# Three plain attention batches ahead of the feed-forward, the third one's x parked in DRAM, and w_out decoded straight to DRAM

## The chip, the cores and the metric

The kernel runs on one core of a Trainium2 chip. The metric is the device time of one execution in microseconds (us); the kernel before has a median of 1222.8 us over three runs. The engines are TensorE (PE in the profile; its weight loads are PEld), VectorE (DVE), ScalarE (ACT), GpSimd (POOL) and SyncE (SP), which starts most DMAs. Each engine works through its own queue in order. SP is such a queue too: a DMA that waits for something holds back every DMA written behind it.

## The reference

Sigmoid attention over 8 batches of 12 heads, 448 positions of 64 numbers, and a feed-forward on the joined result:

```python
scores = scale * np.matmul(q, k.transpose(0, 1, 3, 2)) - np.log(S)
attn_out = np.matmul(1.0 / (1.0 + np.exp(-scores)), v)           # 8 x 12 x 448 x 64
x = attn_out.transpose(0, 2, 1, 3).reshape(B * S, H * D)          # 3584 x 768
h = x @ w_in                                                      # w_in: 768 x 2048
g = 0.5 * h * (1.0 + erf(h * inv_sqrt2))
out = g @ w_out                                                   # w_out: 2048 x 768
```

q, k and v are float32. The weights arrive as float64 bit patterns and have to be turned into float32 on the chip; the text calls this decoding.

## The kernel before

**Blocks.** The 3584 tokens are done as seven blocks of T = 512: the 448 tokens of one batch and 64 of the eighth, whose x is made first and kept in DRAM (`scr_x`). A block is `ffn1` (L433), the first products h with Gelu: 16 slices `fc` of 18 matmuls each, and `ffn2` (L460), the second products: 6 output slices of 16 steps, each step 3 matmuls, 288 in all. Every product is made of three fp32r matmuls, of high and low parts (`wl xh`, `wh xl`, `wh xh`). So each weight unit is split into high and low by one ACT cast (L226) and one DVE subtraction (L227), into the tile `whl`. There are 16 units of `w_in` (768 columns) and 12 of `w_out` (1024 columns, called out 0 to out 11 here, two to each output slice).

**Attention.** Batches 0 to 2 (`PLAIN = 3`; batch 0 is the eighth batch of the input) are done with plain float32 matmuls (`scores_plain` L333, `values_plain` L349), pair of heads by pair of heads; the later ones with split operands (`scores` L281, `values` L376). Before the first block `attention_first` (L398) does batches 0 and 1, so 12 pairs. The attention of batch t + 2 is mixed into `ffn2` of block t by `window` (L490): it makes some score or value matmuls and then lets so many steps of `ffn2` run (`until`), and so on. The text calls such an excursion of TensorE into attention and back a visit. Batch 2, the last plain one, is done in this way in block 0, in 12 halves of a pair. x of the next block goes to `xh` and `xl`, which `ffn1` has finished reading by then. The tokens of the eighth batch are read back from `scr_x` by `load_tokens` (L371).

**Decoding.** The generator `decoder` (L87) cuts the weights into 40 chunks: 16 of w_in, one to a unit (768 KB of float64 each), then 24 of w_out, two to a unit (512 KB). For a chunk i it does `start(i)` (three DVE instructions, L117 to L122), `scale(i)` (two on ACT, L130 and L133) and, one chunk later, `end(i)` (two on DVE, L138 and L147, the last of which writes the float32 weights). Straight after `end(i - 1)` it asks for the raw data of chunk i + 2 (L110, on SP); there are three raw buffers. `W.decode(n)` moves the generator on to two half steps for each chunk of n. After `decode(n)` chunk n - 1 is started and chunk n - 2 ended. Three numbers set the pace, `PACE_A, PACE_F, PACE_W = 14, 8, 24`: 14 during `attention_first`, 8 during the first `ffn1`, the rest during block 0's window. The float32 units of w_in stand in the buffers that g takes later (`first_w`), those of w_out in the three buffers of the tag `wst`. In block 0 both are split from there. They are also stored to DRAM (`scr_in` by SP, `scr_out` by POOL, L190, a whole unit at a time), from where the later blocks read them back into `wst` (`load_to`, L197 to L212).

**Order of preparing.** `prepare_to` (L214) splits the next unit; with the beginning of unit u, unit u + 1 is split, into the buffer that unit u - 1 has just left (`whl` has two in block 0). So the ACT cast of unit u + 1 waits until TensorE has finished unit u - 1, and TensorE waits at the beginning of unit u + 1 for the DVE subtraction. In DVE's queue this subtraction stands between the decoding steps written before and behind it.

Of the kernel before, what the change touches and what calls it, by code (L numbers as in the profile page):

```python
# [17 lines left out]
P = 128  # L18
# [4 lines left out]
def tile_sigmoid_attention_gelu_ffn(  # L23
# [45 lines left out]
    scr_out = tc.dram_tile([NO, P, NFH * P], F32, name="scr_out")  # L69
    scr_x = tc.dram_tile([2, P, NPAIR, S], F32, name="scr_x")  # L70
    WU = max(NC, NFH) * P


    PLAIN = 3
    PACE_A, PACE_F, PACE_W = 14, 8, 24
    SUB_IN, SUB_OUT = NC * P, NFH * P // 2
    SUB = max(SUB_IN, SUB_OUT)
    KEPT = 4
# [8 lines left out]
    def decoder():  # L87
# [47 lines left out]
        def end(i):  # L135
            high = raws.pop(i)[:, :, 1]
            m, e = parts.pop(i)
            nc.vector.scalar_tensor_tensor(  # L138
                e, high, 0x80000000, e, op0=ALU.bitwise_and, op1=ALU.bitwise_or
            )  # L140
            kind, u, c0, w = chunks[i]
            if c0 == 0 and kind == "in":
                first_w[kind, u] = g_tile(u, f"w_in{u}", F32).rearrange("p a b -> p (a b)")
            elif c0 == 0:
                first_w[kind, u] = sb.tile([P, WU], F32, tag="wst", name=f"w_out{u}", bufs=WST)
            t = first_w[kind, u][:, c0 : c0 + w]
            nc.vector.scalar_tensor_tensor(  # L147
                t, m, 2.0**-31, e.bitcast(F32), op0=ALU.mult, op1=ALU.mult
            )

        load(0)
# [14 lines left out]
    class Weights:  # L166
# [9 lines left out]
        def decode(self, n):  # L176

            while self.steps < 2 * n:
                if next(self.decoder, False):
                    self.decoded += 1  # L180
                    if UNITS[self.decoded - 1][0] == "out":
                        self.store_to(self.decoded)
                self.steps += 1

        def store(self):

            kind, u = UNITS[self.stored]
            t = first_w[kind, u]
            dma = (nc.sync if kind == "in" else nc.gpsimd).dma_start
            dma((scr_in if kind == "in" else scr_out)[u], t[:, : width(kind)])  # L190
            self.stored += 1

        def store_to(self, n):
            while self.stored < min(n, self.decoded):
                self.store()

        def load_to(self, n):  # L197

            while self.loaded < min(n, len(self.units)):
                i = self.loaded  # L200
                b, kind, u = self.units[i]
                while self.decoded < min(i + 1, len(UNITS)):
                    self.decode((self.steps + 1) / 2)
                if b == 0:
                    t = first_w[kind, u]
                else:
                    t = sb.tile([P, WU], F32, tag="wst", name=f"wst{i}", bufs=WST)
                    nc.sync.dma_start(
                        t[:, : width(kind)], (scr_in if kind == "in" else scr_out)[u]
                    )  # L210
                self.staged[i] = t
                self.loaded += 1  # L212

        def prepare_to(self, n):  # L214

            while self.ready < min(n, len(self.units)):
# [12 lines left out]
                self.ready += 1  # L229
                self.load_to(i + WST if i + WST >= len(UNITS) else 0)  # L230

# [117 lines left out]
    def values_plain(n):  # L349
# [3 lines left out]
        for c in range(4):  # L353
            a = attn.pop((n, c))
            for j in range(2):
                nc.tensor.matmul(  # L356
                    pav[rows(j), :S], vr[:, j, c], a[:, j], start=c == 0, stop=c == 3
                )
        if b > 0:
            th, tl = xh[:, hp, :S], xl[:, hp, :S]  # L360
# [5 lines left out]
        nc.vector.tensor_tensor(tl, pav[:, :S], th, op=ALU.subtract)  # L366
        if b == 0:
            nc.sync.dma_start(scr_x[0, :, hp], th.bitcast(F32))
            nc.sync.dma_start(scr_x[1, :, hp], tl.bitcast(F32))

    def load_tokens(t):  # L371

        for n, x in enumerate((xh, xl)):
            nc.sync.dma_start(x[:, :, S:].bitcast(F32), scr_x[n, :, :, t * TOK : (t + 1) * TOK])

# [22 lines left out]
    def attention_first():  # L398

        total = 2 * NPAIR  # L400
        load_plain(0)
# [88 lines left out]
    def window(att, ffn):  # L490
# [12 lines left out]
        if att < PLAIN:  # L503
            total -= KEPT
            for n in range(att * NPAIR, (att + 1) * NPAIR):
                for half in range(2):
                    share = (2 * (n % NPAIR) + half + 1) / (2 * NPAIR)
                    for c in range(2 * half, 2 * half + 2):
                        scores_plain(n, c)
                    if half == 1 and n % NPAIR:  # L510
                        values_plain(n - 1)
                    for part in 0.75, 0.5, 0.25, 0:
                        W.decode(PACE_A + PACE_F + PACE_W * (share - part / (2 * NPAIR)))
                        until(share - part / (2 * NPAIR))
                load_plain(n + 3)
            total += KEPT
            until(1)
            values_plain(n)
        elif att < B:
# [19 lines left out]
    with psum("ps_sc0", 3) as ps_sc, psum("ps_av0", 2) as ps_av:  # L539
        attention_first()  # L540
    ps_f = ctx.enter_context(psum("ps_f", 2))
    with psum("ps_sc1", 2) as ps_sc, psum("ps_av1", 2) as ps_av:
        ffn1(0)
        window(2, 0)
    ps_sc, ps_av = (ctx.enter_context(psum(*pool)) for pool in (("ps_sc", 1), ("ps_av", 4)))
    for t in range(1, NB):
        ffn1(t)
# [34 lines left out]
```

## Time and profile before

| | |
|---|---|
| median of three runs (lowest to highest) | 1222.8 us (1222.7 to 1224.67) |
| the profiled execution: its time, its span | 1225.91 us, 1224.1 us |
| instructions on TensorE | 5448 matmuls, 5448 weight loads |
| busy DVE, ACT, POOL | 769.2, 815.5, 8.6 us |
| DMA | 172.23 MB, mean 141 GB/s |
| granted TensorE clock | 0.998 |

A line of a timeline gives the start in us from the beginning of the span, the duration, engine, source line, operation, the tiles as out<-in, shapes and count, and in brackets the idle time ahead of it with what ended it. Matmuls overlap in the pipeline, so that a duration of 0.39 us is not the time from one to the next. A row of the table by windows gives the stretch, its length, for each engine the busy us and the count, then the granted clock, the DMA engines' busy share and GB/s. An issue of a DMA is listed with its size and the time from issue to landing.

### The profile page before, as it was taken

How to read it: one execution, taken by the hardware profiler on the slowest of the kernel's cores; microseconds unless marked ns; L12 is line 12 of the kernel's file. 1: busy time of each engine (PE TensorE's matmuls, PEld its weight loads, DVE VectorE, ACT ScalarE, POOL GpSimd, SP SyncE). 2: the span in 40 equal slices, each digit the busy share in tenths (PEclk: the TensorE clock that was granted, in tenths of full speed). 3: DMA queues.
4: the chain of work that ended last, by engine and by line, in shares of the span. 5: the costliest groups of instructions: out<-in, count | busy, mean ns of one | idle time of the engine just before them, and what ended most of it. 6: DMA issues, size and time to landing. Idle time of an engine off the chain costs nothing.

```text
span 1224.1 us, 15057 instructions
## 1 busy us (share of the span) xinstructions
PE 1210.4 (99%) x5448; PEld 961.8 (79%) x5448; DVE 769.2 (63%) x1127; ACT 815.5 (67%) x1247; POOL 8.6 (1%) x18
## 2 busy tenths in 40 slices
PE   8999999999999999999999999999999999999998
PEld 4338866668888888888888888888888888888887
DVE  4777788623589734798445896447984378953420
ACT  7886576534699744899546997459984489954421
POOL 0000000000000000000000000000000000000000
PEclk9999999999999999999999999999999999999999
DMA  8994567524443135442244432345422544223330
GB/s 278 300 283 153 183 214 246 183 82 154 154 140 113 57 104 174 150 143 73 91 157 147 142 108 76 123 145 162 133 69 87 172 148 147 78 82 104 131 114 26
DMA packets 79881, 172.23 MB, mean 141 GB/s; under 512 B 24256, under 2 KB 39616, under 8 KB 79808
## 3 DMA queue, kind: packets, MB, share of 16 engines
q1 hardware_dynamic: 78080, 164.99, 42.4%
q0 software_dynamic: 1728, 6.29, 1.3%
q8 instruction: 43, 0.70, 0.2%
q14 instruction: 30, 0.25, 0.1%
HBM read 144.90 MB, written 26.35 MB: 140 GB/s over the span
## 4 chain that ended last, share of the span: by engine, by line
PE 95%; DMA 3%; DVE 1%; ACT 1%; SPq 0%; issue 0%; DVEq 0%; ACTq 0%
PE po L477 13%; PE po L478 13%; PE po L479 12%; PE ph L428 12%; PE ph L429 12%; PE ph L430 12%; PE pav L386 7%; PE sc L294 6%; PE pav L356 3%; PE sc L340 3%; DMA raw_ring<-w_in_dram 1%; PE sc_l L289 1%; DMA raw<-w_in_dram 1%; DMA qr<-q_dram 1%; DVE me_ring L117 0%; SPq L328 0%
## 5 line engine op out<-in xcount | busy, mean ns | idle before, releaser
L477 PE MATMUL po<-g,whl 128*128 128x512 f32 x672 | 263.3, 392 | 0.0
L478 PE MATMUL po<-g,whl 128*128 128x512 f32 x672 | 262.3, 390 | 0.0
L479 PE MATMUL po<-g,whl 128*128 128x512 f32 x672 | 261.9, 390 | 0.0
L428 PE MATMUL ph<-xh,whl 128*128 128x512 f32 x672 | 261.5, 389 | 0.0
L429 PE MATMUL ph<-xl,whl 128*128 128x512 f32 x672 | 261.4, 389 | 0.0
L430 PE MATMUL ph<-xh,whl 128*128 128x512 f32 x672 | 261.4, 389 | 0.0
L227 DVE TENSOR_TENSOR whl<-wst,whl 128x768 fp32r<-128x768 f32 (+1 forms) x168 | 179.6, 1072 | 65.1 <-ACT whl L226 61.9
L447 DVE TENSOR_TENSOR g<-gf,g 128x512 fp32r<-128x512 f32 x112 | 77.5, 692 | 212.0 <-ACT g L446 211.8
L445 ACT ACTIVATE gf<-ph 128x512 f32<-128x512 f32 x112 | 66.9, 597 | 199.4 <-PE ph L430 185.5
L226 ACT CAST whl<-wst 128x768 fp32r<-128x768 f32 (+1 forms) x168 | 155.4, 928 | 5.5 <-PE po L479 4.2
L477 PEld LDWEIGHTS po<-g,whl 128*128 128x128 f32 x672 | 126.2, 188 | 31.9 <-issue 8.1
L428 PEld LDWEIGHTS ph<-xh,whl 128*128 128x128 f32 x672 | 126.1, 188 | 26.9 <-issue 0.7
L479 PEld LDWEIGHTS po<-g,whl 128*128 128x128 f32 x672 | 126.1, 188 | 26.8
L430 PEld LDWEIGHTS ph<-xh,whl 128*128 128x128 f32 x672 | 126.1, 188 | 26.2
L429 PEld LDWEIGHTS ph<-xl,whl 128*128 128x128 f32 x672 | 126.1, 188 | 26.1
L478 PEld LDWEIGHTS po<-g,whl 128*128 128x128 f32 x672 | 126.2, 188 | 23.8
L314 ACT ACTIVATE a<-sc 128x896 f32<-128x896 f32 (+1 forms) x174 | 128.3, 786 | 17.3 <-PE sc L340 8.3
L308 DVE TENSOR_TENSOR al<-a,ah 128x896 fp32r<-128x896 f32 x120 | 97.8, 855 | 35.4 <-ACT ah L307 35.4
L307 ACT CAST ah<-a 128x896 fp32r<-128x896 f32 x120 | 85.7, 754 | 5.6 <-PE pav L386 4.2
L386 PE MATMUL pav<-ah,vs 128*128 128x448 f32 x240 | 87.7, 365 | 0.0
L294 PE MATMUL sc<-qs,ks 128*128 128x448 f32 x360 | 82.9, 366 | 0.0
L294 PEld LDWEIGHTS sc<-qs,ks 128*128 128x128 f32 x360 | 67.6, 188 | 6.8
(60 smaller groups left out, 1210.4 us busy)
## 6 DMA issues: line engine op xcount, KB each, us to landing
wst<-scr_in SPq DMA_DIRECT2D x96, 384.0 KB, 3.1
wst<-scr_out SPq DMA_DIRECT2D x72, 512.0 KB, 3.3
kr<-k_dram SPq DMA_DIRECT2D x30, 448.0 KB, 4.3
vr<-v_dram SPq DMA_DIRECT2D x48, 256.0 KB, 4.6
out_dram<-ob SPq DMA_DIRECT2D x42, 224.0 KB, 2.0
raw_ring<-w_in_dram SPq DMA_DIRECT2D x11, 768.0 KB, 7.0
raw_ring<-w_out_dram SPq DMA_DIRECT2D x16, 512.0 KB, 4.7
qr<-q_dram SPq DMA_DIRECT2D x36, 224.0 KB, 3.2
```

What stands on the lines that cost most here:

```text
L226: nc.scalar.copy(hl[:, 0, :w], t[:, :w])
L227: nc.vector.tensor_tensor(hl[:, 1, :w], t[:, :w], hl[:, 0, :w], op=ALU.subtract)
L294: nc.tensor.matmul(o, ks[:, keys], qs, start=n == 0, stop=n == 1)
L308: nc.vector.tensor_tensor(al[t][:, c], a[t][:, c], ah[t][:, c], op=ALU.subtract)
L314: nc.scalar.activation(a, sc, AF.Sigmoid, bias=NEG_LOG_S, scale=SCALE)
L386: nc.tensor.matmul(pav[:, :S], vs[:, j, c], a, start=n == 0, stop=n == len(terms) - 1)
L428: nc.tensor.matmul(ph, wl, xh[:, cc], start=cc == 0, stop=False)
L429: nc.tensor.matmul(ph, wh, xl[:, cc], start=False, stop=False)
L430: nc.tensor.matmul(ph, wh, xh[:, cc], start=False, stop=cc == NC - 1)
L477: nc.tensor.matmul(po, wl, g[fc][:, 0], start=first, stop=False)
L478: nc.tensor.matmul(po, wh, g[fc][:, 1], start=False, stop=False)
L479: nc.tensor.matmul(po, wh, g[fc][:, 0], start=False, stop=last)
```

## The change

1. `attention_first` does all three plain batches, 18 pairs. x of batch 1 goes to `xh` and `xl` as before; x of batches 0 and 2 goes to DRAM, each to a tensor of its own.
2. The window of block 0 makes no attention. It first reads batch 2's x from DRAM into `xh` and `xl` (two DMAs of 128 x 6 x 448 numbers each, on SP, behind the two of `load_tokens`), and then runs `ffn2` with a call of `W.decode` after each step.
3. A decoded chunk of w_out goes to a small tile (tag `al`, three buffers) and from there at once to `scr_out`, 256 KB at a time, by POOL. Block 0 reads its w_out units back into `wst` by SP like the other blocks: out i + 1 is asked for when out i is split.
4. The pace is 15, 11, 18. So with the start of block 0's window 26 chunks are started and 25 ended, where it was 22 and 21.
5. The PSUM buffers have their later layout from block 0 on.

```diff
--- before.py
+++ after.py
@@ -67,12 +67,12 @@
     scr_in = tc.dram_tile([NF, P, NC * P], F32, name="scr_in")
     scr_out = tc.dram_tile([NO, P, NFH * P], F32, name="scr_out")
-    scr_x = tc.dram_tile([2, P, NPAIR, S], F32, name="scr_x")
+    scr_x = {a: tc.dram_tile([2, P, NPAIR, S], F32, name=f"scr_x{a}") for a in (0, 2)}
     WU = max(NC, NFH) * P
     PLAIN = 3
-    PACE_A, PACE_F, PACE_W = 14, 8, 24
+    PACE_A, PACE_F, PACE_W = 15, 11, 18
     SUB_IN, SUB_OUT = NC * P, NFH * P // 2
     SUB = max(SUB_IN, SUB_OUT)
     KEPT = 4
@@ -139,14 +139,17 @@
                 e, high, 0x80000000, e, op0=ALU.bitwise_and, op1=ALU.bitwise_or
             )
             kind, u, c0, w = chunks[i]
-            if c0 == 0 and kind == "in":
-                first_w[kind, u] = g_tile(u, f"w_in{u}", F32).rearrange("p a b -> p (a b)")
-            elif c0 == 0:
-                first_w[kind, u] = sb.tile([P, WU], F32, tag="wst", name=f"w_out{u}", bufs=WST)
-            t = first_w[kind, u][:, c0 : c0 + w]
+            if kind == "in":
+                if c0 == 0:
+                    first_w[u] = g_tile(u, f"w_in{u}", F32).rearrange("p a b -> p (a b)")
+                t = first_w[u][:, c0 : c0 + w]
+            else:
+                t = sb.tile([P, SUB_OUT], F32, tag="al", name=f"w_out{u}_{c0}", bufs=3)
             nc.vector.scalar_tensor_tensor(
                 t, m, 2.0**-31, e.bitcast(F32), op0=ALU.mult, op1=ALU.mult
             )
+            if kind == "out":
+                nc.gpsimd.dma_start(scr_out[u][:, c0 : c0 + w], t)
         load(0)
         load(1)
@@ -178,21 +181,14 @@
             while self.steps < 2 * n:
                 if next(self.decoder, False):
                     self.decoded += 1
-                    if UNITS[self.decoded - 1][0] == "out":
-                        self.store_to(self.decoded)
                 self.steps += 1
-        def store(self):
-
-            kind, u = UNITS[self.stored]
-            t = first_w[kind, u]
-            dma = (nc.sync if kind == "in" else nc.gpsimd).dma_start
-            dma((scr_in if kind == "in" else scr_out)[u], t[:, : width(kind)])
-            self.stored += 1
-
         def store_to(self, n):
-            while self.stored < min(n, self.decoded):
-                self.store()
+
+            while self.stored < min(n, NF):
+                u = self.stored
+                nc.sync.dma_start(scr_in[u], first_w[u][:, : width("in")])
+                self.stored += 1
         def load_to(self, n):
@@ -201,8 +197,8 @@
                 b, kind, u = self.units[i]
                 while self.decoded < min(i + 1, len(UNITS)):
                     self.decode((self.steps + 1) / 2)
-                if b == 0:
-                    t = first_w[kind, u]
+                if b == 0 and kind == "in":
+                    t = first_w[u]
                 else:
                     t = sb.tile([P, WU], F32, tag="wst", name=f"wst{i}", bufs=WST)
                     nc.sync.dma_start(
@@ -227,7 +223,7 @@
                 nc.vector.tensor_tensor(hl[:, 1, :w], t[:, :w], hl[:, 0, :w], op=ALU.subtract)
                 self.split[i] = hl
                 self.ready += 1
-                self.load_to(i + WST if i + WST >= len(UNITS) else 0)
+                self.load_to(i + WST if i >= len(UNITS) else i + 2 if i + 2 > NF else 0)
         def get(self, key):
             i = self.pos[key]
@@ -356,7 +352,7 @@
                 nc.tensor.matmul(
                     pav[rows(j), :S], vr[:, j, c], a[:, j], start=c == 0, stop=c == 3
                 )
-        if b > 0:
+        if b == 1:
             th, tl = xh[:, hp, :S], xl[:, hp, :S]
         else:
             th, tl = (
@@ -364,14 +360,14 @@
             )
         nc.scalar.copy(th, pav[:, :S])
         nc.vector.tensor_tensor(tl, pav[:, :S], th, op=ALU.subtract)
-        if b == 0:
-            nc.sync.dma_start(scr_x[0, :, hp], th.bitcast(F32))
-            nc.sync.dma_start(scr_x[1, :, hp], tl.bitcast(F32))
+        if b != 1:
+            nc.sync.dma_start(scr_x[b][0, :, hp], th.bitcast(F32))
+            nc.sync.dma_start(scr_x[b][1, :, hp], tl.bitcast(F32))
     def load_tokens(t):
         for n, x in enumerate((xh, xl)):
-            nc.sync.dma_start(x[:, :, S:].bitcast(F32), scr_x[n, :, :, t * TOK : (t + 1) * TOK])
+            nc.sync.dma_start(x[:, :, S:].bitcast(F32), scr_x[0][n, :, :, t * TOK : (t + 1) * TOK])
     def values(b, h):
         hp, j = divmod(h, 2)
@@ -397,7 +393,8 @@
     def attention_first():
-        total = 2 * NPAIR
+
+        total = PLAIN * NPAIR
         load_plain(0)
         load_plain(1)
         W.decode(0)
@@ -501,21 +498,12 @@
                 done += 1
         if att < PLAIN:
-            total -= KEPT
-            for n in range(att * NPAIR, (att + 1) * NPAIR):
-                for half in range(2):
-                    share = (2 * (n % NPAIR) + half + 1) / (2 * NPAIR)
-                    for c in range(2 * half, 2 * half + 2):
-                        scores_plain(n, c)
-                    if half == 1 and n % NPAIR:
-                        values_plain(n - 1)
-                    for part in 0.75, 0.5, 0.25, 0:
-                        W.decode(PACE_A + PACE_F + PACE_W * (share - part / (2 * NPAIR)))
-                        until(share - part / (2 * NPAIR))
-                load_plain(n + 3)
-            total += KEPT
-            until(1)
-            values_plain(n)
+            for n, x in enumerate((xh, xl)):
+                nc.sync.dma_start(x[:, :, :S].bitcast(F32), scr_x[att][n])
+            while done < total:
+                next(work)
+                done += 1
+                W.decode(PACE_A + PACE_F + PACE_W * done / total)
         elif att < B:
             for h in range(NH):
                 if h > 0 and h % 2 == 0:
@@ -538,12 +526,10 @@
         nc.gpsimd.memset(a[: S % P], 0.0)
     with psum("ps_sc0", 3) as ps_sc, psum("ps_av0", 2) as ps_av:
         attention_first()
-    ps_f = ctx.enter_context(psum("ps_f", 2))
-    with psum("ps_sc1", 2) as ps_sc, psum("ps_av1", 2) as ps_av:
-        ffn1(0)
-        window(2, 0)
-    ps_sc, ps_av = (ctx.enter_context(psum(*pool)) for pool in (("ps_sc", 1), ("ps_av", 4)))
-    for t in range(1, NB):
+    ps_f, ps_sc, ps_av = (
+        ctx.enter_context(psum(*pool)) for pool in (("ps_f", 2), ("ps_sc", 1), ("ps_av", 4))
+    )
+    for t in range(NB):
         ffn1(t)
         window(t + 2, t)
```

## The prediction

> **What bounds the kernel now.** I read the page first, then the timeline of TensorE through attention_first and block 0, the waits, the table by windows, and the queues of DVE and SP around the two places that the change touches.
>
> ```profile
> span 1224.1 us, 15057 instructions
> PE 1210.4 (99%) x5448; PEld 961.8 (79%) x5448; DVE 769.2 (63%) x1127; ACT 815.5 (67%) x1247; POOL 8.6 (1%) x18
> ...
> DMA  8994567524443135442244432345422544223330
> ...
> q1 hardware_dynamic: 78080, 164.99, 42.4%
> ```
>
> TensorE is busy for 99% of the span, and the change leaves its matmuls as they are. So it can win only what TensorE loses to gaps, half clock and visits, and it can lose by new gaps. The DMA row shows where to look: 9 tenths at the very beginning, 2 to 5 in the later blocks. The queue line gives a price for moved data: 164.99 MB in 42.4% of 1224.1 us is 318 GB/s while all engines are busy.
>
> ```profile
> 4.10 8.71 PE L340 MATMUL sc<-qk 64*128 64x448 f32 x32 [4.10 <-DMA qk<-k_dram]
> ...
> 30.15 3.28 PE L340 MATMUL sc<-qk 64*128 64x448 f32 x16
> ...
> 36.51 3.28 PE L340 MATMUL sc<-qr,kr 64*128 64x448 f32 x16
> ...
> 54.04 1.02 PE L340 MATMUL sc<-qk 64*128 64x448 f32 x4 [2.27 <-ACT a L314]
> ...
> 83.17 1.74 PE L340 MATMUL sc<-qr,kr 64*128 64x448 f32 x4 [2.35 <-ACT a L314]
> ...
> 91.94 0.50 PE L428 MATMUL ph<-xh,whl 128*128 128x512 f32 x1
> ...
> 157.44 1.02 PE L340 MATMUL sc<-qk 64*128 64x448 f32 x4
> ...
> 264.93 0.39 PE L428 MATMUL ph<-xh,whl 128*128 128x512 f32 x1
> ```
>
> A pair of heads takes 36.51 - 30.15 = 6.36 us where nothing disturbs it. Twelve are 76.3 us, and attention_first takes 91.94 - 4.10 = 87.84 us, so 11.5 us are lost in it. Until 30.15 the ideal is four score and three value groups, 7 x 3.18 = 22.3 us; 26.05 passed, so 3.75 us belong to the beginning and 7.8 us come later, in pieces such as the gaps of 2.27 and 2.35 us. ffn1 of block 0 takes 65.5 us for 288 matmuls. The window takes 107.5 us for 288 more of the same shape, taken at 65.5 too, and six pairs (38.2 us), so its visits cost 107.5 - 65.5 - 38.2 = 3.8 us.
>
> ```profile
> 78.70 0.56 DVE L117 TENSOR_SCALAR me_ring<-raw_ring 128x768 uint32<-128x768 uint32 x1 [1.66 <-DMA raw_ring<-w_in_dram]
> 79.29 0.84 ACT L130 ACTIVATE me_ring<-me_ring 128x768 f32<-128x768 int32 x1 [1.18 <-DVE me_ring L117]
> DVE me_ring L117 <- DMA raw_ring<-w_in_dram: 20.2, 7, 11.0
> 30.00:40.00 10.00, 10.00 (x52) 4.12 (x52) 7.86 (x12) 8.63 (x12) 0.00 (x0) 1.00 0.96 314
> 83.40:86.60 3.20, 3.20 (x10) 0.89 (x10) 3.17 (x5) 3.14 (x5) 0.00 (x0) 0.50 0.97 372
> ```
>
> The gaps are told by the first rows: DVE waits for raw weights, ACT's scaling waits for DVE, and the sigmoids that free TensorE's PSUM stand behind it in ACT's queue. DVE lost 20.2 us to this. The raw data are late since the DMA engines are full, 0.96 busy with 314 GB/s. The last row is the aftermath: after the 2.35 us gap the granted clock is 0.50 for over 3.2 us.
>
> **The first stage after the change.** Eighteen pairs share 15 chunks instead of 12 pairs 14: 0.83 a pair against 1.17.
>
> ```profile
> raw_ring<-w_in_dram SPq DMA_DIRECT2D x11, 768.0 KB, 7.0
> wst<-scr_out SPq DMA_DIRECT2D x72, 512.0 KB, 3.3
> scr_out<-w_out POOLq DMA_DIRECT2D x12, 512.0 KB, 4.3
> raw_ring<-w_out_dram SPq DMA_DIRECT2D x16, 512.0 KB, 4.7
> out_dram<-ob SPq DMA_DIRECT2D x42, 224.0 KB, 2.0
> scr_x<-xh SPq DMA_DIRECT2D x6, 224.0 KB, 6.7
> xh<-scr_x SPq DMA_DIRECT2D x7, 192.0 KB, 5.1
> ```
>
> The 0.33 chunk less is 0.26 MB in 6.36 us, 41 GB/s off a load of 314, and two scalings of 0.84 us less a third of a time on ACT. Batch 2 stores its x as batch 0 did. So the later losses should nearly go: I take 0.5 us, between none and 11.6 us (the old rate, 7.8 x 18 / 12), near none because of the undisturbed pairs at 314 GB/s. The beginning keeps its 3.75 us, since the same reads come in the same order. The stage ends at 4.1 + 18 x 6.36 + 3.75 + 0.5 = 122.85, 30.9 us later than before. The window without visits is 65.5 us, 42.0 less. Sum so far: **-11.1 us**. PSUM's layout and the parking stores cost nothing as long as each has a pair's 6.36 us to finish in; uncovered, a store would hold ACT's copy for the 2 us or so that it exceeds that (landing 6.7).
>
> ```profile
> L447 DVE TENSOR_TENSOR g<-gf,g 128x512 fp32r<-128x512 f32 x16 | 11.1, 691 | 1.7 <-ACT g L446 1.4
> L226 ACT CAST whl<-w_out 128x1024 fp32r<-128x1024 f32 x12 | 12.5, 1042 | 6.9 <-PE po L479 3.8 <-PE ph L430 3.1
> L227 DVE TENSOR_TENSOR whl<-w_out,whl 128x1024 fp32r<-128x1024 f32 x12 | 14.7, 1224 | 7.4 <-ACT whl L226 7.4
> L227 DVE TENSOR_TENSOR whl<-w_in,whl 128x768 fp32r<-128x768 f32 x14 | 13.4, 958 | 13.8 <-ACT whl L226 13.8
> ...
> 161.09 0.69 DVE L147 SCALAR_TENSOR_TENSOR w_out<-me_ring 128x512 f32<-128x512 uint32 x1
> ...
> 165.32 0.43 DVE L117 TENSOR_SCALAR me_ring<-raw 128x512 uint32<-128x512 uint32 x1 [0.69 <-DMA raw<-w_out_dram]
> ...
> 169.55 0.43 DVE L117 TENSOR_SCALAR me_ring<-raw_ring 128x512 uint32<-128x512 uint32 x1 [1.41 <-DMA raw_ring<-w_out_dram]
> ...
> 188.28 1.23 DVE L227 TENSOR_TENSOR whl<-w_out,whl 128x1024 fp32r<-128x1024 f32 x1
> 189.42 0.42 DVE L117 TENSOR_SCALAR me_ring<-raw 128x512 uint32<-128x512 uint32 x1
> ...
> 190.82 0.69 DVE L138 SCALAR_TENSOR_TENSOR me_ring<-raw_ring,me_ring 128x512 uint32<-128x512 uint32 x1
> ...
> 192.26 0.43 DVE L117 TENSOR_SCALAR me_ring<-raw_ring 128x512 uint32<-128x512 uint32 x1
> ```
>
> On DVE a start takes 190.82 - 189.42 = 1.40 us, an end 1.44, a split of a w_out unit 1.14 before the next instruction begins. ffn1 of block 0 has 11 chunks in 16 slices: 0.69 x 2.84 + 0.96 + 0.69 = 3.6 us of DVE in a slice of 4.09. It is covered, and costs nothing; uncovered it would cost the excess over 4.09, 16 times.
>
> **The window, where the new waits are.** Let T = 0 be the end of ffn1. A unit of w_out then lasts 65.5 / 12 = 5.46 us on TensorE. DVE comes out of ffn1 at about T = 4.3, as before (161.09 + 0.69 - 157.44), with 25 chunks ended. Left to it are 15 ends and 14 starts, with the splits of out 2 to out 10 between them: 21.6 + 19.6 + 10.3 = 51.5 us, so T = 55.8 without any wait. Out 11 is wanted at 11 x 5.46 = 60.1. There are three kinds of wait.
>
> ```profile
> 161.08 0.33 SPq L110 DMA_DIRECT2D raw<-w_out_dram  x1
> 161.46 0.56 SPq L374 DMA_DIRECT2D xh<-scr_x  x1
> 162.08 0.64 SPq L374 DMA_DIRECT2D xl<-scr_x  x1
> 163.94 3.84 SPq L110 DMA_DIRECT2D raw_ring<-w_out_dram  x2
> ...
> 233.48 0.53 POOL L190 DMA_DIRECT2D scr_out<-w_out  x1 [5.10 <-DVE w_out L147]
> ```
>
> *The read of x.* In SP's queue the token loads came at T = 4.0 and 4.6, behind one raw load, and 0.39 MB of them made the next raw load take 5.6 us (163.94, the first of two in its row, to 169.55) where the one ahead took 4.2 (161.08 to 165.32): DVE lost 1.41 us. Now 2 x 6 x 224 KB = 2.75 MB follow there, and SP's reads are served in turn. Behind them stand raw 28, raw 29 and out 3 (1.57 MB), ahead raw 27 and the tokens (0.92 MB); POOL stores three chunks meanwhile (0.79 MB). 6.03 MB at 318 GB/s are 19.0 us; from 4.0 and with 1.5 us of tail (3.3 us landing less 1.65 of transfer) out 3 lands at 24.5. Cast (1.04) and split (1.22) make it 26.9 before unit 3 begins, instead of 16.4. DVE waits meanwhile in start 28, which it could do at 12.5, until 21.4; behind it in its queue stand end 27 and the split of out 3, for which TensorE waits. At 372 GB/s, the rate of the row at 83.40, this is 2.8 us less. The Trainium skill ("HBM Reference", Specifications (TRN2)) says that a core that streams alone gets about 425 GB/s; by that it would be 4.8 us less. No stretch of 3 us quoted here does, so the sum keeps 318.
>
> *The decoding.* From 26.9 to the end of chunk 37 DVE has 10 ends, 9 starts and 5 splits, 32.7 us. A raw load is asked for at an end and used one start, one end and perhaps a split later, 2.84 to 3.98 us, against a landing of 4.3 to 4.7: about 1.5 us of waits in all. Chunk 37 ends at 61.1. If landing grows to 6 us, since the window asks for some 1.1 MB a chunk, this is 5 to 8 us more; below 3.9 it is 1.5 less.
>
> *The way through DRAM.* An end of a chunk, the store, SP's wait for it, the read back. The store is 256 KB; its nearest rows are 2.0 us (224 KB by SP) and 4.3 (512 KB by POOL); I take 2.8 with the hand-over, and 3.2 for the read: 6.0, between 5.0 and 7.6. POOL starts 24 stores instead of 12, 0.53 us each, with nothing else to do. Behind SP's waiting read stand output stores, for which nobody waits. Out 10 lands at 67.1 and is split at 69.4, where TensorE could go on at about 66.4. The end of chunk 39 stands behind that split in DVE's queue: 70.8. Out 11 is back at 76.8 and split at **79.1**, 19.0 us after 60.1. TensorE stands still for 4.2 us ahead of it, and comes back at half clock: 3.4 us at half speed, 1.7 us. After the first gap the same loss is swallowed, since the decoding is later anyway.
>
> Sum: -11.1 + 19.0 + 1.7 = **+9.6 us**: the profiled execution goes from 1225.9 to 1235.5 us (its span from 1224.1 to 1233.7). It lies 3.1 us above the median of the runs, so I put the median from 1222.8 to **1232**.
>
> **Rivals.** *The reads are not held up* (faster). If the DMA engines serve raw loads beside x, or everything at 372 GB/s or more with landings of 3.8 us, start 28 waits for nothing. DVE then ends chunk 39 at about 59.6 with the out 10 wait counted, and out 11 is split at 67.5: 7.4 us of gap, -11.1 + 7.4 = -3.7, 1219 us. This decides if raw 28 lands before T = 12.5. For it speaks only that peak rates exist; against it the 5.6 us behind the tokens. The Trainium skill ("DMA: Bandwidth & Descriptors", Queues, rings and completion order) says that a DMA engine takes the descriptors of one queue's ring in their order; by that no raw load passes x, and only the rate is left, as the trace's 5.6 us have it too.
>
> *Half of it* (no change). x is read fast, 372 GB/s, and the way through DRAM costs 5.0: out 11 at about 72, 12 us of gap, and the clock holds because the gap is short: +1, 1223 us. For it: after 2.27 us of gap at 54.04 the next four matmuls took 1.02 us, full speed.
>
> *The queue is full throughout* (much slower). Landing of 6 us for all raw loads: chunk 37 some 7 to 8 us later, +18, 1241 us. For it: the first stage shows 7.0 us for 768 KB loads at 314 GB/s; against it: TensorE's waiting itself thins the demand.
>
> *The first stage gains nothing*: if the losses there are ACT's own order and not DMA, 18 pairs lose 11.6 us instead of 0.5, and the sum is +20, 1243 us. Against it: DVE's 20.2 us of waiting for raw data.
>
> **How the numbers follow.** The forecast has 0.50, for 1225 to 1237; faster 0.22, for 1214 to 1220; no change 0.14; the two much slower ones 0.14 together. The range of 8 in 10 is 1217 to 1241: about 1 in 10 lies on each side. A measurement can tell 0.2%, 2.4 us. Slower than that is 0.64, within it 0.14, faster 0.22.
>
> **What would show it.** In the profile after: the first matmul of ffn1 near 123; hardly a wait of DVE for w_in; ffn2's first matmul near 188.5 and no sc or pav in it; a wait of DVE of 7 to 9 us for raw w_out some 12 us later; TensorE idle for over 6 us ahead of the third or fourth unit and for about 4 ahead of the last, both with the clock at 0.50 behind them; ffn1 of block 1 near 274.5. I am wrong if the window takes under 77 us, or if attention_first ends after 130.

## The result and the profile after

| | before | after | forecast for after |
|---|---|---|---|
| median of the runs | 1222.87 us (1222.7 to 1224.67, 4 runs) | 1240.28 us (1239.96 to 1240.85, 4 runs) | 1232, range 1217 to 1241 |
| profiled execution, its span | 1225.91, 1224.1 us | 1240.85, 1239.1 us | 1235.5, 1233.7 us |

The change made the kernel slower: ratio 1.0149, 95% interval [1.0134, 1.0163], +17.4 us by the medians where +9.2 was forecast, +14.9 between the profiled executions where +9.6 was. The direction and the place are those of the forecast; the loss is almost twice as large.

The page after, the lines that answer to those of before:

```profile
span 1239.1 us, 15176 instructions
PE 1212.4 (98%) x5448; PEld 967.7 (78%) x5448; DVE 768.7 (62%) x1127; ACT 812.8 (66%) x1245; POOL 15.5 (1%) x30
...
DMA  8876577764444225442245431344422454223330
...
q1 hardware_dynamic: 83104, 176.78, 43.9%
...
L474 PE MATMUL po<-g,whl 128*128 128x512 f32 x672 | 265.3, 395 | 18.0 <-DVE whl L223 18.0
```

Apart from GpSimd, which issues twice as many stores, no engine does noticeably more than before. What is new is the last number: 18.0 us in which TensorE waited at `ffn2` for a subtraction of the weights' split. The timeline of TensorE shows where (L336 is a score of the plain batches, L425 `ffn1`, L474 `ffn2`):

```profile
42.20 3.28 PE L336 MATMUL sc<-qk 64*128 64x448 f32 x16
48.56 3.28 PE L336 MATMUL sc<-qk 64*128 64x448 f32 x16
...
121.58 0.50 PE L425 MATMUL ph<-xh,whl 128*128 128x512 f32 x1
...
187.68 0.39 PE L427 MATMUL ph<-xh,whl 128*128 128x512 f32 x1
190.10 0.47 PE L474 MATMUL po<-g,whl 128*128 128x512 f32 x1 [2.03 <-DVE whl L223]
...
204.51 0.50 PE L474 MATMUL po<-g,whl 128*128 128x512 f32 x1 [1.65 <-DVE whl L223]
...
218.35 0.80 PE L474 MATMUL po<-g,whl 128*128 128x512 f32 x1 [8.06 <-DVE whl L223]
...
232.20 0.50 PE L474 MATMUL po<-g,whl 128*128 128x512 f32 x1 [1.04 <-DVE whl L223]
...
245.24 0.50 PE L474 MATMUL po<-g,whl 128*128 128x512 f32 x1 [1.82 <-DVE whl L223]
...
261.40 0.50 PE L474 MATMUL po<-g,whl 128*128 128x512 f32 x1 [3.39 <-DVE whl L223]
...
279.48 0.39 PE L425 MATMUL ph<-xh,whl 128*128 128x512 f32 x1
```

The pairs run at 6.36 us once the beginning is over, and the first stage ends at 121.58. `ffn1` takes 66.1 us to 187.7. Then six waits stand in the window, 18.0 us in all, not the two that the prediction named as its signs, and block 1 begins at 279.48 instead of the forecast's 274.5. The table by windows gives the rest of the loss:

```profile
190.10:279.50 89.40, 73.44 (x289) 58.44 (x290) 57.40 (x91) 34.17 (x49) 9.04 (x16) 0.90 0.73 250
...
218.40:222.00 3.60, 3.60 (x9) 2.83 (x10) 3.46 (x7) 1.85 (x3) 0.62 (x1) 0.51 0.98 350
```

From its first matmul on, the window takes 89.4 us and TensorE is busy for 73.4 of it. 289 matmuls take 65.5 us undisturbed, so 16.0 us are waits and 7.9 us are slow matmuls: behind four of the six waits the granted clock falls (0.51 in the second row: 9 matmuls in 3.60 us).

Two chains lie behind these waits. The first is the forecast's read of x, in DVE's and SP's queue:

```profile
203.24 1.22 DVE L223 TENSOR_TENSOR whl<-wst,whl 128x1024 fp32r<-128x1024 f32 x1
212.82 0.43 DVE L117 TENSOR_SCALAR me_ring<-raw_ring 128x512 uint32<-128x512 uint32 x1 [8.36 <-DMA raw_ring<-w_out_dram]
...
197.77 1.11 SPq L502 DMA_DIRECT2D xh<-scr_x  x1
198.93 2.88 SPq L502 DMA_DIRECT2D xl<-scr_x  x1
201.90 1.02 SPq L110 DMA_DIRECT2D raw_ring<-w_out_dram  x1
```

The raw chunk 28 is asked for behind x, and DVE waits 8.36 us in its beginning. The second chain is the way of a unit through DRAM. It stands in the view of the critical chain (start, duration, what) ahead of the wait of 3.39 us at 261.40, and in DVE's timeline around it:

```profile
249.66 5.32 DMA scr_out<-w_out
255.04 3.98 DMA wst<-scr_out
259.05 1.05 ACT whl L222
260.12 1.24 DVE whl L223
261.40 0.50 PE po L474
```

```profile
232.78 0.69 DVE L148 SCALAR_TENSOR_TENSOR w_out<-me_ring 128x512 f32<-128x512 uint32 x1
...
243.96 1.23 DVE L223 TENSOR_TENSOR whl<-wst,whl 128x1024 fp32r<-128x1024 f32 x1 [1.64 <-ACT whl L222]
...
248.67 0.69 DVE L148 SCALAR_TENSOR_TENSOR w_out<-me_ring 128x512 f32<-128x512 uint32 x1
...
260.12 1.23 DVE L223 TENSOR_TENSOR whl<-wst,whl 128x1024 fp32r<-128x1024 f32 x1 [2.32 <-ACT whl L222]
261.26 0.42 DVE L117 TENSOR_SCALAR me_ring<-raw_ring 128x512 uint32<-128x512 uint32 x1
...
264.71 0.69 DVE L148 SCALAR_TENSOR_TENSOR w_out<-me_ring 128x512 f32<-128x512 uint32 x1
```

This is a loop. Out 7's second half (a half is one chunk) is written at 233.47, and the unit's split ends 11.7 us later. Behind that split in DVE's queue stand the ends of out 9's two halves, the second written at 249.36; its way is 12.0 us, and behind its split stand the ends of out 11's halves, written at 265.40. So two units go round in 16 us, where TensorE needs 10.9 for them. DVE's own work on two units (four starts, four ends, two splits) is 13.6 us by the prediction's prices; this too is more than 10.9, so DVE depends on the chunks decoded ahead of the window.

The waits of the whole program and the DMA issues from 187 to 280 us carry the sizes:

```profile
ACT whl L222 <- DMA wst<-scr_out: 21.8, 9, 3.5
...
SPq L204 <- DMA scr_out<-w_out: 29.6, 6, 6.0
```

```profile
raw_ring<-w_out_dram SPq DMA_DIRECT2D x9, 512.0 KB, 5.4
wst<-scr_out SPq DMA_DIRECT2D x9, 512.0 KB, 4.3
scr_out<-w_out POOLq DMA_DIRECT2D x16, 256.0 KB, 5.3
```

### The profile page after: what moved, and what is told of

It is laid out like the page before. It is cut to its first block, busy times and chain, and to the rows that moved or that the text cites. A ratio compares the mean times of both kernels' runs of the same rounds, so it can differ in the third digit from the quotient of the medians.

```text
span 1239.1 us, 15176 instructions
## 1 busy us (share of the span) xinstructions
PE 1212.4 (98%) x5448; PEld 967.7 (78%) x5448; DVE 768.7 (62%) x1127; ACT 812.8 (66%) x1245; POOL 15.5 (1%) x30
## 4 chain that ended last, share of the span: by engine, by line
PE 91%; issue 5%; DMA 1%; DVE 1%; POOL 1%; ACT 1%; SPq 0%; POOLq 0%; DVEq 0%; ACTq 0%
PE ph L427 12%; PE ph L425 12%; PE ph L426 12%; PE po L475 11%; PE po L474 11%; PE po L476 11%; PE pav L382 7%; PE sc L290 6%; PE sc L336 5%; PE pav L352 4%; PE sc_l L285 1%; POOL scr_out L152 1%; DMA scr_out<-w_out 0%; DMA wst<-scr_out 0%; DMA scr_x<-xh 0%
## 5 line engine op out<-in xcount | busy, mean ns | idle before, releaser
L474 PE MATMUL po<-g,whl 128*128 128x512 f32 x672 | 265.3, 395 | 18.0 <-DVE whl L223 18.0
L425 PE MATMUL ph<-xh,whl 128*128 128x512 f32 x672 | 261.7, 389 | 0.6 <-DVE whl L223 0.6
L223 DVE TENSOR_TENSOR whl<-wst,whl 128x768 fp32r<-128x768 f32 (+1 forms) x180 | 194.3, 1082 | 81.8 <-ACT whl L222 78.7
L442 ACT ACTIVATE gf<-ph 128x512 f32<-128x512 f32 x112 | 66.9, 598 | 200.8 <-PE ph L427 186.9
L222 ACT CAST whl<-wst 128x768 fp32r<-128x768 f32 (+1 forms) x180 | 167.9, 936 | 25.0 <-DMA wst<-scr_out 21.8
L474 PEld LDWEIGHTS po<-g,whl 128*128 128x128 f32 x672 | 127.8, 190 | 44.4 <-DVE whl L223 18.1
L476 PEld LDWEIGHTS po<-g,whl 128*128 128x128 f32 x672 | 127.7, 190 | 27.4
L425 PEld LDWEIGHTS ph<-xh,whl 128*128 128x128 f32 x672 | 126.2, 188 | 27.9 <-ACT g L443 1.0
L475 PEld LDWEIGHTS po<-g,whl 128*128 128x128 f32 x672 | 127.9, 190 | 24.6
```

Of the source, the lines that this page charges most:

```text
L222: nc.scalar.copy(hl[:, 0, :w], t[:, :w])
L223: nc.vector.tensor_tensor(hl[:, 1, :w], t[:, :w], hl[:, 0, :w], op=ALU.subtract)
L425: nc.tensor.matmul(ph, wl, xh[:, cc], start=cc == 0, stop=False)
L474: nc.tensor.matmul(po, wl, g[fc][:, 0], start=first, stop=False)
L475: nc.tensor.matmul(po, wh, g[fc][:, 1], start=False, stop=False)
L476: nc.tensor.matmul(po, wh, g[fc][:, 0], start=False, stop=last)
```

## The experiments

In the expectations theory 1 is the read of x, which keeps the raw weights back. Theory 2 is at first that the decoding is the limit whatever x does, and from the fifth run on the way of each unit through DRAM: its store, the read of it into `wst` (the read-back), cast and split. Each edit is against the changed kernel unless said otherwise; each time is compared with runs of the kernel before on the same chip (medians 1221.7 to 1224.0 us).

**x read at the end of the window.**

```diff
-            for n, x in enumerate((xh, xl)):
-                nc.sync.dma_start(x[:, :, :S].bitcast(F32), scr_x[att][n])
             while done < total:
+                if done == 73:
+                    for n, x in enumerate((xh, xl)):
+                        nc.sync.dma_start(x[:, :, :S].bitcast(F32), scr_x[att][n])
```

> The changed kernel with one thing moved: the two reads of batch 2's x are asked for before step 73 of the 96 steps of block 0's second products, instead of before the first. In the changed kernel raw chunk 28 took 10.8 us to land behind them, DVE waited 8.36 us for it and TensorE 8.06 us ahead of out 3. Theory 1 (the reads of x stand in front of the others in SP's queue, and all that follows is late by that): both waits go, nothing takes their place, the window of 91.9 us becomes about 84, and the kernel takes 1232 us. Theory 2 (the decoding is the limit anyway and later waits take the place of this one): DVE's other waits for raw data and read-backs grow by half of it or more, and the time falls by 4 us or less, to 1236 to 1239.

1241.41 us, ratio 1.0157 [1.0127, 1.0186]: no gain, and outside both expectations. The 8.36 us of DVE are gone (its waits for `raw_ring<-w_out_dram` are 3.0 us in 3, the longest 1.3), yet TensorE still stops five times in the window, the longest 4.89 us. The read costs something at its new place too: block 1 then starts with a wait of 2.54 us, and ACT waits 8.7 us for a w_in unit. So this run alone doesn't price x, but x can't be the whole.

**x issued by ScalarE's queue**, `nc.scalar.dma_start` for the two reads, at the old place.

> The changed kernel with the two reads of batch 2's x issued by ACT at the same place in the program, so that they stand in another queue than the raw and w_out reads, on the same DMA engines. Theory 1 in its strict form (the order within SP's queue is what costs): raw 28 lands in 4 to 6 us instead of 10.8, DVE waits for it 1 to 3 us, the gap ahead of out 3 shrinks from 8.06 to about 2, and the kernel takes about 1234 us. Rival (the engines' rate is what costs, about 400 GB/s in this stretch, whatever the queue): raw 28 still takes 9 us or more and the time stays within 2 us of 1240.

1241.17 us, 1.0155 [1.0125, 1.0184]. DVE's waits for those raw chunks are 10.0 us in 4 (9.3 in 2 before), the gap is 8.02 us and has moved one unit ahead. Raw chunk 28 took 13.0 us to land, not less than the 10.8 behind x in SP's queue. So the rival is borne out: what delays the raw data beside x is mainly the transfers themselves, not SP's order.

**The first two read-backs one slice earlier.**

```diff
-                self.load_to(i + WST if i >= len(UNITS) else i + 2 if i + 2 > NF else 0)
+                ahead = 3 if i < NF else 2
+                self.load_to(i + WST if i >= len(UNITS) else i + ahead if i + ahead > NF else 0)
```

> The changed kernel with out 0 and out 1 read back one slice of the first products earlier. In the changed kernel the read of out 0 landed 7.6 us after its issue; TensorE waited 2.03 us for it at the beginning of the second products, went on at half clock for 3.4 us, and DVE came to the end of chunk 24 at 9.0 us after the first products, where I had 4.3. Theory A (this wait, which the prediction left out, shifts the whole decoding): the gap and the half clock go, DVE is back at about 5 us, and the kernel takes 1235.5 us. Theory B (the reads of x decide when raw 28 comes, and they are asked for at the same place in DVE's work either way, so only TensorE's own 2 to 4 us at the beginning are saved and the gap ahead of out 3 grows by as much): within 1.5 us of 1240.

1238.33 us, 1.0132 [1.0102, 1.0161], between the two theories and nearer to B. The wait at `ffn2`'s beginning is gone, but the six that are left make 17.6 us, hardly less than the 18.0 before; 8.69 of them stand ahead of out 3. The beginning is worth 2 us.

**Three more chunks decoded in `ffn1`**: pace 15, 14, 15.

> The changed kernel with the pace 15, 14, 15 instead of 15, 11, 18: three more chunks of w_out are decoded during the first products. DVE was busy for 51.0 of the 65.6 us there; three chunks are 8.5 us more. If the lateness of the decoding is what sets the end of the window (theory 2, and theory 1 beside it), all of 8 us come off: 1232 us. If the way through DRAM and the read of x set it by themselves, at most 2 us. If DVE has no room in a slice (14/16 of 2.84 and 1.65 us make 4.13 of 4.09 us), the first products become up to 3 us longer, which would be seen as gaps between the slices.

1234.26 us, 1.0098 [1.0069, 1.0128]: 6 us back, less than the 8 of the first case and more than the 2 of the second. The last chunk ends 66.9 us after `ffn2`'s first matmul instead of 75.3, but gaps of 1.82, 2.56, 5.89 and 2.05 us are left. A later start of the loop helps, and doesn't cure it.

**No read of x**: the two lines are left out, so that block 1 works on batch 1's x again.

> The changed kernel without the two reads of batch 2's x: block 1 then multiplies batch 1's x once more, so the second block's columns are not the reference's; the work on the engines is the same. It settles what the late reads left open, where the reads stood in front of block 1's weights instead. Theory 1 (the reads of x cost 8 us, and only their new place hid it): 1232 us. Theory 2, as it stands after the first four runs (each unit of w_out waits for its own store and read back, 5.3 us of store, about 4.5 of read, 2.3 of cast and split after the end of its second chunk, and DVE's next chunks and SP's next raw reads stand behind that): the wait for raw 28 goes, chunk 39 ends only about 3 us earlier, as in the run with late reads (72.1 against 75.3 us after the window's beginning), and the kernel takes 1236 to 1238 us.

1236.47 us, 1.0122 [1.0101, 1.0142], as theory 2 had it: 0.0027 or some 3 us better than the changed kernel, and the intervals overlap. What TensorE waits for without x (its timeline in this run):

```profile
204.95 0.80 PE L474 MATMUL po<-g,whl 128*128 128x512 f32 x1 [3.88 <-DVE whl L223]
...
226.55 0.50 PE L474 MATMUL po<-g,whl 128*128 128x512 f32 x1 [3.02 <-DVE whl L223]
240.89 0.50 PE L474 MATMUL po<-g,whl 128*128 128x512 f32 x1 [3.17 <-DVE whl L223]
256.89 0.80 PE L474 MATMUL po<-g,whl 128*128 128x512 f32 x1 [3.22 <-DVE whl L223]
```

The one long gap is gone, and a gap of 3 to 4 us at every second or third unit takes its place: the loop, the last three of them 14 and 16 us apart.

**Block 0 without the way through DRAM.** The halves are kept and split from SBUF, each half by itself; DRAM is written only for the later blocks. Pace and x are as in the changed kernel.

```diff
-                t = sb.tile([P, SUB_OUT], F32, tag="al", name=f"w_out{u}_{c0}", bufs=3)
+                if u % 6 > 2:
+                    tag = ("al", "ah")[c0 > 0]
+                    t = sb.tile([P, SUB_OUT], F32, tag=tag, name=f"w_out{u}_{c0}", bufs=3)
+                else:
+                    if c0 == 0:
+                        first_w["out", u] = sb.tile([P, WU], F32, tag="wst", name=f"w_out{u}", bufs=WST)
+                    t = first_w["out", u][:, c0 : c0 + w]
+                halves.setdefault(u, []).append(t)
...
-                if b == 0 and kind == "in":
-                    t = first_w[u]
+                if b == 0:
+                    t = [first_w[u][:, : width(kind)]] if kind == "in" else halves[u]
...
```

> The changed kernel with the way through DRAM undone for block 0: the decoded chunks of w_out stay in SBUF (units 0 to 2 and 6 to 8 in the three wst buffers, the others as halves in the six buffers that the plain attention has left), are split from there, and are stored to DRAM for the later blocks only. Pace and the read of x as in the changed kernel. Theory 2: no split waits for a read any more; the gap of 2.0 us at the beginning with its half clock and most gaps at units go; what is left is the wait for raw 28 (about 8 us, now hidden from TensorE at out 3 and found again at the end) and DVE's 56 us of work: out 11 is split at about 70 us instead of 84, and the kernel takes 1224 to 1227 us. Theory 1 (x alone): the gap ahead of out 3 stays at 6 to 8 us and the kernel takes 1234 or more.

1226.45 us, 1.0040 [1.0025, 1.0054], as theory 2 had it. This removes 0.0109, 13 us, of the loss, and all the small gaps but one of 0.43 us; the gap of x is left, 8.51 us:

```profile
213.55 0.79 PE L485 MATMUL po<-g,whl 128*128 128x512 f32 x1 [8.51 <-DVE whl L234]
```

The edit also takes the twelve read-backs off the DMA engines, and raw loads (`raw_ring`) land in 4.4 us instead of 5.4. That isn't where the 13 us come from, as far as the raw data go: DVE's waits for raw w_out only fall from 12.2 to 10.8 us.

**The same with x late.**

> The kernel of the direct run with the reads of x asked for before step 73. Theory 2 with the read of x as the second term: raw 28 no longer waits, chunk 39 ends 60 to 62 us after the window's beginning, out 11 is ready at 63, 2 to 4 us late, and the kernel takes 1216 to 1219 us, 7 us less than with the reads at the beginning. If the decoding hides the reads of x there: the same time as the direct run within 2 us.

1218.84 us, 0.9975 [0.9965, 0.9984], as theory 2 had it: faster than before, and all gaps of the window together are about 3 us. Here, with the other chain gone, moving x is worth 7.6 us; in the changed kernel it was worth nothing.

**Halves from SBUF, x at the beginning, pace 18, 12, 14.**

> The kernel of the direct run with the pace 18, 12, 14: 18 chunks during the attention, 12 in the first products, so that 31 chunks are started at the beginning of the window, not 26. DVE then has some 31 us of decoding and 11 us of splits in 65.5 us, and the units stand three ahead, so an 8 us wait for raw data is covered. Expected: no gap of TensorE in the window, which takes 65.5 to 67 us, the first stage 1 chunk a pair and not slower than 123 us; 1214 us, below both kernels. If the DMA engines cannot carry one chunk a pair beside the attention, the first stage shows gaps again and loses 3 to 6 us of it: 1217 to 1220.

1222.90 us, 1.0010 [1.0001, 1.0019]; the expectation was 8.9 us too low. Its reason, that units decoded three ahead cover the read of x, was wrong. DVE's timeline in this run:

```profile
199.85 0.69 DVE L155 SCALAR_TENSOR_TENSOR w_out<-me_ring 128x512 f32<-128x512 uint32 x1
208.38 0.43 DVE L117 TENSOR_SCALAR me_ring<-raw 128x512 uint32<-128x512 uint32 x1 [7.84 <-DMA raw<-w_out_dram]
208.72 0.42 DVE L119 TENSOR_SCALAR me_ring<-raw 128x512 uint32<-128x512 uint32 x1
209.18 0.69 DVE L122 SCALAR_TENSOR_TENSOR me_ring<-raw,me_ring 128x512 uint32<-128x512 uint32 x1
209.79 1.29 DVE L234 TENSOR_TENSOR whl<-w_out,whl 128x512 fp32r<-128x512 f32 x2
```

The split at 209.79 is that of out 3, whose second half was written at 164.70, 45 us earlier. It stands behind the beginning of a later chunk, whose raw data come late behind x. Being ahead in data was no cover here, since the queue's order is fixed.

**Both: pace 18, 12, 14 and x late.**

> Both cures together: block 0's halves of w_out are split from SBUF, the decoding is spread 18, 12, 14, and the two reads of x are issued before step 73. With x at the beginning, the window had one gap of 6.14 us and the half clock behind it, and was 74.0 us long. Theory that the way through DRAM and the read of x are all that the window lacks: no gap over 1 us, window 66 to 67 us, time 1214 to 1216. Rival, the split of a unit that is already decoded still stands in VectorE's queue behind the beginning of a later chunk whose raw read is late, x or no x: gaps of 2 to 5 us stay, time 1218 to 1222, no better than the halves from SBUF with x late and the spread of the changed kernel (1218.8).

1214.37 us (1213.93 to 1214.89), 0.9925 [0.9910, 0.9939]. It beats both kernels. The window in this run, by the table:

```profile
187.30:252.80 65.50, 65.50 (x289) 53.94 (x288) 46.77 (x82) 29.99 (x52) 7.50 (x13) 1.00 0.67 219
```

TensorE is busy for the whole 65.5 us, at full clock. The first theory holds, its rival doesn't. This is the window that the change could have had.

**The read-backs issued by GpSimd**, so that no raw read stands behind a read-back that waits in SP's queue; first with x in its place, then with x late.

```diff
-                    nc.sync.dma_start(
+                    (nc.gpsimd if b == 0 else nc.sync).dma_start(
```

> The changed kernel with one edit: block 0's read-backs of w_out are issued by GpSimd behind its stores, not by SP, so that no raw read stands behind a waiting read-back in SP's queue (there 29.6 us in 6 waits). Theory that SP's order carries the loss: the raw reads behind come 4 to 5 us earlier each, the sum of the gaps in the window falls from 18 to some 10 us, time 1230 to 1234. Rival, the serial way of a unit (store 5.3 us at the median, read-back, cast, split) carries it whoever issues the read: gaps stay within 3 us of 18, time 1237 to 1241; it would show as ScalarE's waits for the read-back staying near 3.5 us each.

1246.15 us, 1.0184 [1.0167, 1.0201]: worse than the changed kernel, and above both expectations.

> The same with the two reads of x before step 73. Where SP's order carried the loss, both late reads are now gone from it: time 1225 to 1230. Where the serial way of a unit carries it: 1235 to 1240, since moving x alone left 1241.

1242.67 us, 1.0160 [1.0143, 1.0178], again above both, and about that of x late alone (1.0157). What SP's order would have given for the two, 1230 to 1234 and 1225 to 1230, did not come. The waits from 120 to 282 us in the last run:

```profile
ACT whl L222 <- DMA wst<-scr_out: 34.7, 8, 6.9
...
PE po L474 <- DVE whl L223: 20.7, 8, 7.3
...
DVE me_ring L117 <- DMA raw<-w_out_dram: 2.9, 3, 1.4
```

DVE waits little for raw chunks (2.9 us, and 1.8 more for those in `raw_ring`; with x late alone the two were 6.1), and TensorE waits more than with x late alone, 20.7 us against 14.0, with ACT's casts waiting 34.7 us for read-backs. So the way of the unit itself costs, whoever issues the read. The size was missed here too: it grew where GpSimd issued the reads. Probably a read-back that waits in GpSimd's queue holds the next halves' stores (in the last run POOL waited 16.2 us for stores in 4 read-backs); this was not tried by itself.

## Why the prediction was right in direction and wrong in size

*The gains were right.* The first stage ended at 121.58, forecast 122.85: its losses went, as DVE's waits for raw data had promised. Beyond the first chunk these fell from 15.1 to 4.3 us in this stage. That a parking store could cost "2 us or so" did not follow from its own numbers (6.7 less 6.36 is 0.3); the pairs show no such cost. Without visits or waits the window is 65.5 us, as the run with both chains removed shows, which decodes at another pace too; its gain is 0.0075, 9.2 us, near the -11.1 of the first two terms.

*The read of x was sized rightly, but its weight was not.* DVE lost 8.36 us, forecast 8.9 (from 12.5 to 21.4). It came 4.3 us later than forecast, since DVE could have begun chunk 28 at 204.5, 16.8 us after `ffn1`, and not at 12.5. And it is only in part a loss of its own: some 3 us in the changed kernel, 7.6 with the way through DRAM gone.

*The step that failed is the way through DRAM.* The prediction took 6.0 us for store and read-back, "between 5.0 and 7.6", and charged it for the last two units only, out 10 and out 11; for the time from 26.9 to the end of chunk 37 it counted 32.7 us of DVE's work and 1.5 of waits for raw loads, none for read-backs. Measured, for out 7 and out 9: 11.7 and 12.0 us from the end of a chunk to the end of the split, of which the store of out 9 took 5.3 and its read-back 4.0, against the forecast's 8.3. More than the size, its place in the order was missed. Chunk ends stand behind a split in DVE's queue all through the window, so the way is paid at every second unit: 16 us for two units. Unit 3 began 30.7 us after `ffn1` (forecast 26.9), chunk 37 ended at 70.1 (61.1). Between the two DVE did the forecast's 32.7 us of work; the rest is 4.0 us of waits for late splits, where the forecast had none, and 2.9 for raw loads (1.5). With all that hangs on it, the way is worth the 13 us that the run without it gained.

The end was otherwise than forecast as well. Chunk 39's end stood behind out 9's split, not behind out 10's. Out 11's own way took 8.3 us, as forecast, with little else left to move, and its split ended at 86.0 (79.1):

```profile
267.02 1.23 DVE L223 TENSOR_TENSOR whl<-wst,whl 128x1024 fp32r<-128x1024 f32 x1 [1.61 <-ACT whl L222]
272.44 1.23 DVE L223 TENSOR_TENSOR whl<-wst,whl 128x1024 fp32r<-128x1024 f32 x1 [4.19 <-ACT whl L222]
```

But the wait of 4.2 us ahead of out 11 was not there. TensorE had been held up at out 9, and in the critical chain it comes to out 11 half a us after this split:

```profile
274.20 0.23 PE po L474
```

*Left out altogether*: out 0 and out 1 are read back in the last slices of `ffn1`. ACT's casts wait for these read-backs, 3.50 us for out 0's and 2.82 for out 1's. The first costs the 2.03 us at 190.10, and both bring chunk 24's end from the forecast's T = 4.3 to 9.0.

```profile
187.65 1.05 ACT L222 CAST whl<-wst 128x1024 fp32r<-128x1024 f32 x1 [3.50 <-DMA wst<-scr_out]
```

*The half clock* was counted once, 1.7 us, and came four times, 7.9 us in all. That the earlier ones are "swallowed" fits this trace: the casts of w_out in the window waited for read-backs and never for TensorE, so by these waits the chain that ended at 261.40 doesn't run over TensorE's slow matmuls. From 261.40 three units took 18.1 us to 279.48, where 16.4 are the full clock's: 1.7 us, behind the last wait. The size was right; the place was not, since it was to follow a wait ahead of out 11 and followed that ahead of out 9.

*The statement on SP's queue was wrong.* Behind the waiting read-back (29.6 us in 6 waits) raw loads did stand, not output stores alone. Taking them out of that place gained nothing in the one way that was tried, with GpSimd issuing the read-backs; what it would be worth without GpSimd's own waits stays open.

*From the profile to the median.* The median lies 8.3 us above the forecast. Of these 5.35 stand between the profiled executions too, 1240.85 against 1235.5; block 1 began 5.0 us late. Some 2.5 more are from the step to the median: the profiled execution of before (1225.91) lay 3.1 us above the runs, the changed one (1240.85) 0.6. The rest is the rounding of 1232. The forecast counted the first stage's gaps of that execution as gain (2.35 us and the half clock at 83.17 among them); that the usual execution doesn't have them all was not measured, as only one was profiled.

*The rivals.* "The queue is full throughout" gave 1241 and came nearest, but not by its mechanism: raw loads landed at 5.4 us where it wanted 6, and apart from x DVE waited 3.8 us for them. That its time was met is luck. "The reads are not held up" and "Half of it" had the read of x as the decider; without it the kernel is still 1.0122. "The first stage gains nothing" is refuted by the 121.58.

The Trainium skill ("DMA: Bandwidth & Descriptors", Anatomy of one DMA — SWDGE (gpsimd) path) fits a transfer's time as 2.0 us and its bytes at 436 GB/s. By this, as an estimate, GpSimd's 256 KB store takes 2.6 us. The trace doesn't agree in the loaded window: 5.3 at the median, with the engines 0.73 busy. Only the last store, at 265.70 with little else left to move, took 2.3. The 2.8 us that the prediction took are near the page and far from the loaded window.

## What to carry to other kernels

A result sent through DRAM costs the store's completion and the read's landing in series, and the price is paid each time round if the engine's queue puts the next piece of work behind the consumer of the last: look for that loop (end, store, read, cast, split, next end) and compare its period with TensorE's. Check as well which splits or ends stand behind which all through the stage, not only at its end. Two waits that each delay the same work can't be priced by taking one away: x was worth nothing, 3 or 7.6 us, by what else was late. Being ahead in data helps only if the instruction that uses it isn't queued behind one that waits.

## What the runs showed of the hardware

- Landing times under load: from 187 to 280 us a 256 KB store by GpSimd took 5.3 us at the median, between 2.3 (the last one) and 7.5. In the page of before a 224 KB store by SP took 2.0.
- A wait of 1.82 us at 245.24 was followed by half clock (0.58 from 245.2 to 249.0), one of 1.65 us at 204.51 by full clock. Before, 2.27 us kept the full clock and 2.35 us lost it, so in these rows the length of the wait alone doesn't decide. The Trainium skill ("TensorE: Matmul & The Clock Gate", Part 1) says that the clock falls after an idle window of about 3.4 us which runs freely. A window that runs freely would fit the lack of order in these lengths; that a whole idle window of 3.4 us is needed does not agree with the wait of 1.82 us.
- While x was read, the core moved more than the 318 and 372 GB/s that the prediction took from before. The GB/s row from 187 to 280 us, in 40 slices of 2.3 us:

```profile
GB/s 208 379 155 0 153 222 322 408 402 397 406 284 118 277 330 341 231 381 234 238 186 337 310 234 284 65 287 298 368 55 329 294 109 330 132 238 350 139 119 0
```

  Four slices, from 203 to 213 us, stand at 397 to 408.
